# A block of attention, a token mixer and an MLP on one core: x's tile used again as room, and attention blocks normalised as each ends

## The chip, the core and the metric

The kernel runs on one core of one Trainium2 chip. Five engines work side by side: TensorE (PE in the profile, its weight loads PEld), VectorE (DVE), ScalarE (ACT), GpSimd (POOL) and SyncE (SP), which issues every DMA here. The metric is device time in microseconds (us), the median of several executions; lower is better.

## What is computed

The input x has 2048 tokens of 640 features. Two branches start from its layer norm xn, and both are added to x. All is float32.

```python
qkv = (xn @ wqkv)                       # 32 heads of 20 features
p = softmax(q @ k.T * 20 ** -0.5)       # per head, 2048 x 2048
a = (p @ v) @ wo
h = gelu(xn @ w1)                       # then four groups of columns shifted by +1, -1, +2, -2 tokens
x1 = x + shifted(h) @ w2
b = x1 + gelu(layernorm(x1) @ w3) @ w4  # 1536 hidden features
out = x + a + b
```

## The kernel before

The kernel is written through a planner of its own (class `Plan`): each helper records an operation with its cost, its key (when it is wanted) and what it depends on, and `schedule` then lays all operations on the engines. For TensorE the order is not left to the planner: the string `ORDER` has one letter for each of its 7058 steps, and says of which kind the next one is. The instructions of each engine and of SP's queue then run in that order; an instruction that waits holds up all that stand behind it on its engine.

**Attention (letters m, s, p).** Two heads are a pair, and a pair has two blocks of 1024 queries: 32 blocks (`blk`). A block is 32 units. `max_step` (m) makes scores of 128 queries against 512 keys for both heads, and DVE takes their maximum (`mx<-pm`); `max_fin` turns a block's maxima into two more rows of q's tile, by way of TensorE (`pmt`) and DRAM (`md`). `unit` (s) makes the transposed scores, two products of 62 rows that run side by side; ACT takes exp of each (`p<-s`); every second unit, (p) adds the four products of probabilities and values into `pv`. A quarter of a block's keys is summed in PSUM, copied out by ACT or DVE (`obq<-pv`) and added by POOL (`ob<-ob,obq`). m runs 43 units ahead of s. There are 1024 m, 1024 s and 512 p.

**Dense products (letter d).** All of the projections are filled in between: v, k and q (`psv`, `ps_k`, `ps_q`), w1 (`ps1`), w2 with the residual and the layer norm (`ps2`, transposes `tz`), w3 (`ps3`), w4 (`ps4`) and wo (`pso`, and `psl` for the last rows). Each float32 operand is split in a rounded part and a rest, so a product is three passes. `twins` runs two sums side by side in two halves of TensorE's rows, and changes halves in the middle; between the two turns `fence`, a POOL memset of one element (`scratch`, L334), waits for the last product of the first turn, and the first product of the second turn waits for it.

**Memory.** `xT` holds xn transposed, hi and lo, for all tokens (80 KB of each partition) until the last product of q and w1. `w23_phase` then opens new tiles: `w2s` (w2, later part of w4), `zT` (the second layer norm transposed, half of the tokens at a time, later the rest of w4), and `hs` with the shifted h. `w4_phase` splits a tile `g` of 128 tokens into `gT` for each of 16 sums `ps4_t`. When w4 is through, `wo_phase` opens `wos` (wo), `acc` (the result) and `oc`.

**End of a block.** `block_end` writes a block's sums `ob` to DRAM (`od`), copies the heads' rows to `onm` and the row of denominators to `sm`, takes their reciprocal (`rc<-sm`, DVE), and writes that back (`rcd`) and 20 times over (`rce`). `load_o` in `wo_phase` reads `onm` and `rce`, and POOL or DVE multiplies them (`oc<-oc,rb`).

Of the kernel before, what the change touches and what calls it, by code (L numbers as in the profile page):

```python
# [95 lines left out]
    "dddddddddddddddddddddddddddddddddddddddddddddddddddddddddddddddddddddddddddddddddddddddddddddddddddddddddddddm"  # L96
    "dddddddddddmddddddddddddddddddddddddddddddddddddddddddddddddmddddddddddmmdddddddmdddddmddddddddmddddddddddmddd"
    "ddmdmddddddddmddmddddddddddmdddddddddddmmddddddddddddddddmdmmddddddddddddddmddddddddddddmddddmmddddddddddmdddd"
    "dddddddmdddddmddddmmdddddddddddddddddmdddddmddddddddmmdddddddmddddddddddddmdddddddddmdddmmddddddddddddmddddddd"
    "mdddddddsddsddsdddddddddddddddddddsddddmsdddddddmssdddddddsddmddppppdsdddsddddsdddmdddsddmdddmsdddmdsddddmsddd"  # L100
    "dsdddmmppppmsdddmdmdsddddsddmdsdddsmddddsmddddsmddsddmdddmmppppsmddsddmdsddmddmdsdddmddsmdddddmddddsdmddsdmdmd"
    "dmppmspsmpsmsmssmpsmspsmspmmspsmspmmspsmddddsmddddmdddsdmdddsmdddsdmdddsdmdddsdmdddsppmsmpsmpmmspsdddmddsddddm"
    "dddddmdspdmsddddddmsddddsddmdddmppmdsddddddsddmddddddsmdddddsddmdddsdddddmmppmsddsddddmddsddddmdddsmdddddddsmd"
    "ddsdddddmmppppsmdddsddddmdsdddmddddsmddddddsdmdddsdddmddspmsmpppmsdddsddddmddsddddddsmddddsddmddsdddmddddsmppp"
    "pddssdmddddddddmsdddddmsdddddmddsddmddddmdmdppsmddddddsdmdddddsdmddsddmddddsddmdddddsdmdpssmpsdddmddsddmdddddd"
# [490 lines left out]
def tile_kernel(tc, x, wqkv, wo, w1, w2, w3, w4, out):  # L596
# [401 lines left out]
    def w23_phase():  # L998
# [4 lines left out]
        for k in range(ND):  # L1003
            load_row(w2s, "w2", k)
# [444 lines left out]
```

## Time and profile before

| | us |
|---|---|
| median of 3 runs | 1900.74 |
| the 3 runs | 1896.83 to 1901.31 |
| the profiled execution | 1897.56 |
| its span, first to last instruction | 1895.8 |

The profiled execution took 1.8 us more than its span, and 3.2 us less than the median. The page has busy times by engine and a strip of 40 slices; windows give the same for any stretch; a timeline has instructions in order of time. A busy PE is not PE at its best: a product's end is modelled, and a product that waits inside a run of others still counts as busy. So what PE could do is read from the distances between starts.

### The profile page before, as it was taken

The numbers are of one execution on the slowest core, as the hardware profiler recorded it, in microseconds if no ns is written. First come the engines' busy times: TensorE is split into PE (matmuls) and PEld (weight loads), VectorE is DVE, ScalarE is ACT, GpSimd is POOL, SyncE is SP. The second block draws the span as 40 slices with busy tenths as digits, with TensorE's granted clock in tenths as the row PEclk, the third lists the DMA queues.
The fourth block names the chain that finished last, engine by engine and source line by source line (L and its number), as shares of the span: only waits on it lengthen the run. The fifth ranks groups of instructions, "written<-read, shape, count | busy, mean of one in ns | idle before, by whom it ended". The sixth has DMA issues, their size and how long they took to land.

```text
span 1895.8 us, 44073 instructions
## 1 busy us (share of the span) xinstructions
PE 1871.9 (99%) x17185; PEld 1278.4 (67%) x17185; DVE 1581.2 (83%) x2826; ACT 1340.8 (71%) x2461; POOL 353.9 (19%) x562
## 2 busy tenths in 40 slices
PE   7999999999999999999999999999999999999998
PEld 5975666565656657676666756665777776775677
DVE  8979888888888989988788998778787888788734
ACT  4267767777877885777787667778577776767661
POOL 5001111212112112211112311111122112211221
PEclk9999999999999999999999999999999999999999
DMA  4554545655555466545346573435523232314612
GB/s 173 167 170 146 156 119 135 184 161 180 148 152 149 127 196 220 169 154 169 125 131 219 172 225 105 128 101 162 139 86 107 74 108 86 91 53 156 224 48 112
DMA packets 234375, 271.57 MB, mean 143 GB/s; under 512 B 59006, under 2 KB 174158, under 8 KB 232366
## 3 DMA queue, kind: packets, MB, share of 16 engines
q1 hardware_dynamic: 234166, 268.75, 46.4%
q8 instruction: 135, 2.21, 0.5%
q14 instruction: 74, 0.61, 0.1%
HBM read 162.72 MB, written 115.79 MB: 147 GB/s over the span
## 4 chain that ended last, share of the span: by engine, by line
PE 94%; DVE 3%; DMA 2%; POOL 1%; issue 1%; SPq 0%; ACT 0%; DVEq 0%; POOLq 0%; ACTq 0%
PE ps L346 26%; PE pv L346 24%; PE s L346 14%; PE pm L346 14%; PE psv L346 4%; PE pso L346 3%; PE ps_k L346 3%; PE ps_q L346 3%; DVE mx L316 2%; PE psl L346 1%; DMA wd_w<-ph_w 1%; PE tz L316 1%; PE tp L316 0%; DMA od<-ob 0%; PE pmt L346 0%
## 5 line engine op out<-in xcount | busy, mean ns | idle before, releaser
L316 DVE TENSOR_REDUCE mx<-pm 128x1 f32<-128x512 f32 x2048 | 1282.0, 683 | 195.6 <-PE pm L346 178.8
L316 ACT ACTIVATE p<-s 128x512 f32<-128x512 f32 x2048 | 1084.2, 609 | 293.4 <-PE s L346 249.8
L346 PE MATMUL pv<-p,v 128*32 128x512 f32 x4096 | 494.6, 598 | 0.0
L346 PE MATMUL s<-zq,kpack 62*128 62x512 f32 x2048 | 449.7, 413 | 3.8 <-DVE mx L316 1.5
L346 PE MATMUL pm<-kpack,zq 60*128 60x512 f32 x2048 | 450.6, 413 | 0.5
L346 PEld LDWEIGHTS s<-zq,kpack 62*128 62x128 f32 x2048 | 231.9, 185 | 133.7 <-DVE mx L316 40.9
L346 PEld LDWEIGHTS pm<-kpack,zq 60*128 60x128 f32 x2048 | 229.7, 185 | 124.9 <-DVE mx L316 35.4
L346 PEld LDWEIGHTS pv<-p,v 128*32 128x32 f32 x4096 | 109.6, 109 | 222.2 <-issue 193.2
L346 PE MATMUL ps<-zT,w_w 64*128 64x512 f32 x1440 | 228.6, 394 | 0.0
L316 POOL TENSOR_TENSOR ob<-ob,obq 128x512 f32<-128x512 f32 x96 | 125.0, 1302 | 414.4 <-ACT obq L316 311.1
L346 PEld LDWEIGHTS ps<-zT,w_w 64*128 64x128 f32 x1440 | 150.2, 186 | 21.0 <-POOL scratch L334 1.7
L346 PE MATMUL ps<-zT,gT 64*128 64x320 f32 x1344 | 140.0, 306 | 0.0
L346 PEld LDWEIGHTS ps<-zT,gT 64*128 64x128 f32 x1344 | 124.2, 186 | 4.8
L316 ACT COPY obq<-pv 128x512 f32<-128x512 f32 x77 | 45.2, 588 | 99.6 <-PE pv L346 98.3
L346 PE MATMUL ps<-w2s,gT 64*128 64x320 f32 x960 | 98.2, 307 | 0.0
L346 PE MATMUL ps<-w2s,hs 64*128 64x320 f32 x960 | 96.3, 309 | 0.0
L346 PE MATMUL psv<-wv,xT 64*128 64x320 f32 x960 | 94.6, 314 | 1.6 <-POOL wv L316 1.5
L346 PE MATMUL ps<-xT,w_w 64*128 64x512 f32 x600 | 95.5, 395 | 0.0
L334 POOL MEMSET scratch<- 1x1 f32 x134 | 11.9, 89 | 422.2 <-PE ps L346 227.1
L346 PEld LDWEIGHTS ps<-w2s,gT 64*128 64x128 f32 x960 | 85.3, 186 | 7.7 <-ACT p L316 0.8
L346 PEld LDWEIGHTS psv<-wv,xT 64*128 64x128 f32 x960 | 82.7, 189 | 9.3 <-POOL wv L316 2.2
L346 PEld LDWEIGHTS ps<-w2s,hs 64*128 64x128 f32 x960 | 84.5, 185 | 6.1 <-DVE mx L316 1.7
(173 smaller groups left out, 1498.1 us busy)
## 6 DMA issues: line engine op xcount, KB each, us to landing
zq<-qd SPq DMA_DIRECT2D x156, 80.0 KB
kpack<-kd SPq DMA_DIRECT2D x78, 160.0 KB
w_w<-wd_w SPq DMA_DIRECT2D x48, 256.0 KB
gd<-pre SPq DMA_DIRECT2D x8, 1536.0 KB
g<-gd SPq DMA_DIRECT2D x64, 192.0 KB
wd_w<-ph_w SPq DMA_DIRECT2D x34, 320.0 KB
vd<-vst SPq DMA_DIRECT2D x32, 256.0 KB
kd<-hl_k SPq DMA_DIRECT2D x16, 512.0 KB
```

Source lines behind the costliest of these rows:

```text
L316: getattr(e, m)(val(out), *[val(x) for x in ins], **{k: val(v) for k, v in kw.items()})
L334: o.insts = [nc.gpsimd.memset(scratch.get(), 0.0)]
L346: o.insts = [nc.tensor.matmul(out.get(), lhsT.get(), rhs.get(), **kw) for out, lhsT, rhs, kw in products]
```

## The change

Inputs, products and the number of steps of each kind in `ORDER` stay; the order itself is written anew. The edits are these.

- `xT` stays open to the end of w4. Its first 640 columns of tokens become w2 (`W2`) and later part of w4, the columns 640 to 896 the shifted h of every second pair of tiles, its second half z, the rest of w4 (`w4v`), and the split g of every odd w4 sum. `w2s` and `zT` are gone. For this, the last two dense jobs before w2 (`w1_4` and `q4`) run their halves crosswise, so that the first half of the tokens is read out earlier.
- 15 of w4's 24 pieces (10 before) are loaded ahead of the second half's w3. `g` has one buffer instead of two.
- Four fifths of wo (`wos`) are loaded into `g`'s place once the last g is split, ahead of the last w4 sum's result. The last fifth (`ws4`), `oc` and `acc` come after w4.
- `block_end` writes the four rows of denominators alone (8 KB), reads the reciprocals back spread over 32 partitions each (`rb`, 4 DMAs), POOL multiplies (`rb<-ob,rb`), and 4 DMAs write `onm`. `rce` and the 20 products `oc<-oc,rb` in `wo_phase` are gone.
- `place` and `vst` move to pools that close early.

```diff
-    place = const.tile([P, 2, 2, P], F32R, name="place")
+    lnp = pl.pool(name="lnp", bufs=2)
+    place = lnp.tile([P, 2, 2, P], F32R, name="place")
...
-    od = dt([NPAIR, 2, P, 512], F32, "od")
+    od = dt([NB, 4, 512], F32, "od")
     onm = dt([D, S], F32, "onm")
-    rcd = dt([NB, 2 * HALF], F32, "rcd")
-    rce = dt([D, S], F32, "rce")
+    rcd = dt([NB, 4, 512], F32, "rcd")
     r2d = dt([NT, P], F32, "r2d")
...
+                if room and turn + i == 0:
+                    last.deps.append((room.tile.alloc_op, 1))
...
+    vsp = pl.pool(name="vsp", bufs=1, side="right")
...
+        ends = []
+
+        def run(n, w):
+            f = w1_tile if n[0] == "w" else qk_tile
+            if n not in jobs[-2:]:
+                return f(n, w)
+            ends.append((f, n, w))
+            f(n, w, (0,))
+        ahead(jobs, lambda n: early(w1_load, n) if n[0] == "w" else early(wcol, st1, n), run)
+        for f, n, w in ends:
+            f(n, w, (2,))
         wp.close()
...
+    W2 = [[xT[:, :, k, 320 * n:320 * (n + 1)] for n in range(2)] for k in range(ND)]
+    ZC = S // 2
+    HS = slice(640, 896)
+
...
-        w2p = pl.pool(name="w2p", bufs=1, side="right")
-        w2s = w2p.tile([P, 2, ND, D], F32R, name="w2s")
-        wp = pl.pool(name="ztp", bufs=1, side="right")
-        zT = wp.tile([P, 2, ND, S // 2], F32R, name="zT")
...
+        def hs_load(q):
+            if q % 2 == 0:
+                hs = [xT[:, :, k, HS] for k in range(ND)]
+            else:
+                t = sp.tile([P, 2, ND, 256], F32R, tag="hs", name=f"hs{q}", bufs=1)
+                hs = [t[:, :, k, :] for k in range(ND)]
+            t0 = q * 256
+            edge = {0: 0, NT // 2 - 1: 254}.get(q)
+            for k in range(ND):
+                if edge is None:
+                    dma(_f(hs[k]), _f(hsd[k][:, :, t0:t0 + 256]), 262144)
...
-                pl.renew(w2s)
-                for k in range(ND):
-                    load_row(w2s, "w4", k)
-                gp = pl.pool(name="s4g", bufs=2, side="right")
-                gs = [load_g(gp, t) for t in range(2)]
+                xrp.close()
+                for key in W4_ALL[:3 * ND]:
+                    early(dma, _f(w4v(*key)), _f(wdone["w4_%d_%d" % key]), 327680)
+                gp = pl.pool(name="s4g", bufs=1)
...
+    def w4v(k, n):
+        i = 2 * (k - ND) + n
+        if k < ND:
+            return W2[k][n]
+        if i < ND:
+            return xT[:, :, i, 640:960]
+        i -= ND
+        return xT[:, :, i // 3, ZC + 320 * (i % 3):ZC + 320 * (i % 3 + 1)]
...
+            if t % 2:
+                gT = [[xT[:, p, 3 + k // 6, ZC + k % 6 * P:ZC + (k % 6 + 1) * P] for k in range(NF)] for p in range(2)]
+                split(xT[:, 0, 3:5, ZC:ZC + 768], xT[:, 1, 3:5, ZC:ZC + 768],
+                      g.rearrange("p (a k) t -> p a (k t)", a=2), NF * P)
+            else:
+                gt = sp.tile([P, 2, NF, P], F32R, tag="gT", name=f"gT{t}", bufs=1)
+                split(gt[:, 0], gt[:, 1], g, NF * P)
+                gT = [[gt[:, p, k, :] for k in range(NF)] for p in range(2)]
+            if t + 1 < NT:
+                gs.append(load_g(gp, t + 1))
+            else:
+                gp.close()
+                wp = pl.pool(name="wosp", bufs=1)
+                ws = wp.tile([P, 2, 4, D], F32R, name="wos")
+                for k in range(4):
+                    load_row(ws, "wo", k)
             pss = [pd(f"ps4_{t}_{n}")[:, :320] for n in range(2)]
...
+    def load_o(sp, k, b):
+        m = P if k < 4 else r0
+        oc = sp.tile([P, 512], F32, tag="oc", name=f"oc{k}_{b}", bufs=8)
+        if m < P:
+            pl("pool", 600.0, "memset", oc[64:], 0.0, port=True)
+        dma(oc[:m], onm[k * P:k * P + m, b * 512:(b + 1) * 512], m * 2048)
+        return oc
...
-            for c in range(0, HALF, 512):
-                rb = sp.tile([P, 512], F32, tag="rb", name=f"rb{k}_{half}_{c}", bufs=3)
-                dma(rb[:m], rce[k * P:k * P + m, half * HALF + c:half * HALF + c + 512], m * 2048)
-                pl("pool", c_pool(512), "tensor_mul", oc[:m, c:c + 512], oc[:m, c:c + 512], rb[:m], port=True,
-                   alt=("dve", c_dve(512), "tensor_mul", True))
...
-        adma(od[pair, qh], ob, 262144)
         n = 2 * HALF // P
-        cols = slice(qh * HALF, (qh + 1) * HALF)
-        src = od[pair, qh].rearrange("(q e r) n -> e r q n", e=2, q=2)
-        for e in range(2):
-            h = 2 * pair + e
-            adma(onm[h * DH:(h + 1) * DH, cols].rearrange("r (q n) -> r q n", q=2), src[e, :DH], 81920)
+        adma(od[blk], ob[DH:P:32, :], 8192)
         pl.key += REST
         sm = pp.tile([P, n], F32, tag="sm", name=f"sm{blk}", bufs=2)
-        adma(sm, od[pair, qh].rearrange("(s r) (c n) -> s r c n", r=32, n=n)[:, DH], 8192, LATE)
+        adma(sm, od[blk].rearrange("s (c n) -> (s c) n", n=n), 8192, LATE)
         rc = pp.tile([P, n], F32, tag="rc", name=f"rc{blk}", bufs=2)
         pl("dve", 185.0, "reciprocal", rc, sm)
-        adma(rcd[blk].rearrange("(p n) -> p n", n=n), rc, 8192)
-        src = rcd[blk].rearrange("(q e n) -> e q n", e=2, q=2)
-        for e in range(2):
-            h = 2 * pair + e
-            adma(rce[h * DH:(h + 1) * DH, cols].rearrange("r (q n) -> r q n", q=2),
-                 src[e].unsqueeze(0).to_broadcast([DH, 2, 512]), 81920)
+        adma(rcd[blk].rearrange("s (c n) -> (s c) n", n=n), rc, 8192)
+        rb = pp.tile([P, 512], F32, tag="rb", name=f"rb{blk}", bufs=1)
+        for r in range(4):
+            adma(rb[32 * r:32 * (r + 1), :], rcd[blk, r:r + 1].to_broadcast([32, 512]), 65536)
+        pl("pool", c_pool(512), "tensor_mul", rb, ob, rb, port=True)
+        for r in range(4):
+            h = 2 * pair + r % 2
+            c0 = qh * HALF + r // 2 * 512
+            adma(onm[h * DH:(h + 1) * DH, c0:c0 + 512], rb[32 * r:32 * r + DH, :], 40960)
```

Where the order moves, in the rows of the two built programs. TensorE first, around the end of w4's last sum, `ps4_15`, in the program before: the sum's last row, then attention alone (the number after s is the unit, after pm the step of maxima).

```order
L346 MATMUL ps4_15_0_27265<-zT_11047,gT15_26762 128x320
L346 MATMUL s939_0_27600<-zq2_81,kpack0_77 128x512
L346 MATMUL s939_1_27601<-zq2_81,kpack0_77 128x512
L346 MATMUL s940_0_27604<-zq2_81,kpack0_77 128x512
L346 MATMUL s940_1_27605<-zq2_81,kpack0_77 128x512
```

From here no dense row stands until wo's. In the program before, the same attention runs on to the first product with wo, `pso_0`. The last unit before it is 981, the last step of maxima 1018 (1019 stands two rows behind it).

```order
L346 MATMUL pv30_2_28324<-p978_0_28233,v15_26406 32x512
L346 MATMUL pv30_2_28324<-p979_0_28273,v15_26406 32x512
L346 MATMUL pv30_2_28324<-p978_1_28272,v15_26406 32x512
L346 MATMUL pv30_2_28324<-p979_1_28274,v15_26406 32x512
L346 MATMUL pso_0_0_28345<-wos_27719,oT0_0_27730 128x320
L346 MATMUL pso_0_1_28346<-wos_27719,oT0_0_27730 128x320
```

So 43 units, 939 to 981, stand between the two. The changed program at the end of `ps4_15`, which stands behind unit 942 there:

```order
L346 MATMUL ps4_15_0_27434<-xT_201 128x320
L346 MATMUL pm988_0_27803<-kpack1_77,zq0_78 128x512
L346 MATMUL pm988_1_27804<-kpack1_77,zq0_78 128x512
L346 MATMUL s943_0_27808<-zq2_80,kpack0_76 128x512
L346 MATMUL s943_1_27809<-zq2_80,kpack0_76 128x512
```

The sum has moved behind four more units. And the changed program at the first product with wo:

```order
L346 MATMUL pm1014_0_28422<-kpack1_77,zq1_79 128x512
L346 MATMUL pm1014_1_28423<-kpack1_77,zq1_79 128x512
L346 MATMUL s976_0_28433<-zq0_78,kpack1_77 128x512
L346 MATMUL s976_1_28434<-zq0_78,kpack1_77 128x512
L346 MATMUL pso_0_0_28438<-wos_26986,oT0_0_27942 128x320
L346 MATMUL pso_0_1_28439<-wos_26986,oT0_0_27942 128x320
```

Between the two sums stand 43 s, 32 m and 22 p before, and 34 s, 27 m and 20 p now.

POOL at the end of block 20, before: the last two quarters are added, and two fences and the first quarter of block 21 follow.

```order
L316 TENSOR_TENSOR ob20_18747<-ob20_18747,obq20_2_19898 128x512
L316 TENSOR_TENSOR ob20_18747<-ob20_18747,obq20_3_20021 128x512
L334 MEMSET scratch_67 1x1 x2
L316 TENSOR_TENSOR ob21_19500<-ob21_19500,obq21_1_20179 128x512
L316 TENSOR_SCALAR nm_22_19160<-m8_22_19148 128x16
L316 CAST hr_22_19161<-nm_22_19160 128x16
```

Nothing of block 20 is left to POOL after that until `wo_phase`. And now, for block 20: the product `rb20` stands behind the quarters with a fence ahead of it and one behind it.

```order
L316 TENSOR_TENSOR ob20_19044<-ob20_19044,obq20_2_20020 128x512
L316 TENSOR_TENSOR ob20_19044<-ob20_19044,obq20_3_20136 128x512
L334 MEMSET scratch_67 1x1
L316 TENSOR_TENSOR rb20_19849<-ob20_19044,rb20_19849 128x512
L334 MEMSET scratch_67 1x1
L316 TENSOR_TENSOR ob21_19793<-ob21_19793,obq21_1_20294 128x512
```

Of the 30 products `rb`, 6 have a fence as the next instruction of POOL and 4 more as the next but one.

SP's queue near the end of w4, before: the last result of w4 (`ad` from `r15`) is written, then wo is loaded.

```order
L316 DMA ad_123<-r14_26519 128x640
L316 DMA od_128<-ob28_25644 128x512
L316 DMA onm_129<-od_128 20x2x512 x2
L316 DMA sm28_25785<-od_128 128x1x16
L316 DMA rcd_130<-rc28_25822 128x16
L316 DMA rce_131<-rcd_130 20x2x512 x2
L316 DMA ad_123<-r15_26892 128x640
L316 DMA wos_27719<-wd_wo_0_0_327 128x2x320
L316 DMA wos_27719<-wd_wo_0_1_328 128x2x320
```

All of wo stands behind the results of w4. Now wo's loads stand ahead of the results of sums 14 and 15 (`r15` is only being loaded), and behind block 27's new chain of DMAs, of which the first two rows show the end.

```order
L316 DMA rb27_26066<-rcd_125 32x512 x4
L316 DMA onm_124<-rb27_26066 20x512 x4
L316 DMA ad_118<-r13_26172 128x640
L316 DMA wos_26986<-wd_wo_0_0_327 128x2x320
L316 DMA wos_26986<-wd_wo_0_1_328 128x2x320
L316 DMA wos_26986<-wd_wo_1_0_329 128x2x320
L316 DMA wos_26986<-wd_wo_1_1_330 128x2x320
L316 DMA wos_26986<-wd_wo_2_0_331 128x2x320
L316 DMA wos_26986<-wd_wo_2_1_332 128x2x320
L316 DMA wos_26986<-wd_wo_3_0_333 128x2x320
L316 DMA wos_26986<-wd_wo_3_1_334 128x2x320
L316 DMA r15_27071<-rd_117 128x640
```

Eight loads of wo (four fifths of it) have moved ahead of `r15`; each needs the place of the last g, so SP waits there until g15 is split.

## Rows read from the trace of the kernel before

**Rows 1.** The page: span, busy times, strip of PE's clock, chain.

```profile
span 1895.8 us, 44073 instructions
...
PE 1871.9 (99%) x17185; PEld 1278.4 (67%) x17185; DVE 1581.2 (83%) x2826; ACT 1340.8 (71%) x2461; POOL 353.9 (19%) x562
...
PEclk9999999999999999999999999999999999999999
...
PE 94%; DVE 3%; DMA 2%; POOL 1%; issue 1%; SPq 0%; ACT 0%; DVEq 0%; POOLq 0%; ACTq 0%
```

**Rows 2.** Windows of four stretches, products of s alone: window, length, PE busy (count).

```profile
646.40:657.00 10.60, 3.44 (x12) 1.00 0.51 112
...
1106.20:1118.10 11.90, 4.63 (x22) 1.00 0.86 182
1298.50:1322.40 23.90, 8.45 (x32) 1.00 0.62 213
1721.50:1773.40 51.90, 20.72 (x86) 1.00 0.73 248
```

**Rows 3.** Timeline of PE in the last stretch: start, length, what.

```profile
1747.95 0.39 PE L346 MATMUL pm<-kpack,zq 60*128 60x512 f32 x2
1748.18 0.40 PE L346 MATMUL s<-zq,kpack 62*128 62x512 f32 x2
1748.51 1.06 PE L346 MATMUL pv<-p,v 128*32 128x512 f32 x8
1749.50 0.50 PE L346 MATMUL pm<-kpack,zq 60*128 60x512 f32 x2
```

**Rows 4.** Timeline of PE while w4 runs.

```profile
1500.76 3.64 PE L346 MATMUL pv<-p,v 128*32 128x512 f32 x32
1504.33 0.50 PE L346 MATMUL pm<-kpack,zq 60*128 60x512 f32 x2
```

**Rows 5.** Groups in the stretch 1721.5 to 1773.4: busy us, mean ns | idle before.

```profile
L316 ACT ACTIVATE p<-s 128x512 f32<-128x512 f32 x85 | 43.5, 635 | 6.8 <-PE s L346 5.6 <-PE pv L346 0.8
L316 DVE TENSOR_REDUCE mx<-pm 128x1 f32<-128x512 f32 x65 | 40.2, 680 | 6.8 <-PE pm L346 6.8
L346 PE MATMUL pv<-p,v 128*32 128x512 f32 x176 | 22.4, 602 | 0.0
...
L346 PE MATMUL pm<-kpack,zq 60*128 60x512 f32 x64 | 16.8, 454 | 0.0
```

**Rows 6.** Windows of that stretch and the next: PE, PEld, DVE, ACT, POOL busy.

```profile
1721.50:1773.40 51.90, 51.86 (x330) 20.95 (x326) 44.87 (x77) 46.13 (x92) 8.44 (x10) 1.00 0.73 248
1773.40:1825.30 51.90, 51.90 (x607) 42.31 (x604) 29.41 (x54) 28.13 (x56) 15.83 (x24) 1.00 0.38 129
```

**Rows 7.** Groups of DVE in the same stretch.

```profile
L316 DVE TENSOR_TENSOR oc<-oc,rb 128x512 f32<-128x512 f32 x3 | 2.0, 683 | 0.0
```

**Rows 8.** Groups of POOL over the whole span.

```profile
L316 POOL TENSOR_TENSOR ob<-ob,obq 128x512 f32<-128x512 f32 x96 | 125.0, 1302 | 414.4 <-ACT obq L316 311.1 <-DVE obq L316 94.7 <-DVE ph_wo L316 8.1
L316 POOL TENSOR_TENSOR gT<-g,gT 128x1536 fp32r<-128x1536 f32 x12 | 41.8, 3484 | 136.2 <-ACT gT L316 85.9 <-DMA zq<-qd 28.2 <-DMA g<-gd 11.6
...
L334 POOL MEMSET scratch<- 1x1 f32 x134 | 11.9, 89 | 422.2 <-PE ps L346 227.1 <-PE psv L346 43.6 <-PE pso L346 36.1
```

**Rows 9.** Waits of SP's queue: total, times, longest us.

```profile
SPq L316 <- DMA rcd<-rc: 33.6, 22, 6.2
```

**Rows 10.** Waits of the engines: total, times, longest us.

```profile
POOL scratch L334 <- PE ps L346: 227.1, 48, 18.2
```

**Rows 11.** The page: weight loads of w3's sums, with PE's wait for fences.

```profile
L346 PEld LDWEIGHTS ps<-zT,w_w 64*128 64x128 f32 x1440 | 150.2, 186 | 21.0 <-POOL scratch L334 1.7
```

**Rows 12.** Timeline of DVE and POOL side by side.

```profile
1752.79 1.29 DVE L316 TENSOR_REDUCE mx<-pm 128x1 f32<-128x512 f32 x2 [1.46 <-PE pm L346]
1752.88 1.28 POOL L316 TENSOR_TENSOR ob<-ob,obq 128x512 f32<-128x512 f32 x1 [7.30 <-ACT obq L316]
```

**Rows 13.** Groups of ACT over the whole span.

```profile
L316 ACT CAST gT<-g 128x1536 fp32r<-128x1536 f32 x14 | 20.8, 1482 | 2.0 <-PE ps L346 2.0
```

More of the change, by code (lines that the diff above doesn't have):

```diff
@@ L101 @@
[L101 to L105, printed above, removed]
@@ L708, in parts, with twins @@
         return [(lhs(a, k), rhs(b, k)) for k in kts for a, b in ((0, 0), (0, 1), (1, 0))]
-    def twins(tiles, sums, n, first=0, more=()):
+    def twins(tiles, sums, n, first=0, more=(), room=None):
         last = None
@@ L810, in tile_kernel @@
     vw0 = v_load(0)
-    vst = [pp.tile([P, 8, 2, VC], F32, name=f"vst{i}", tag=f"vst{i}", bufs=1) for i in range(VSB)]
+    vst = [vsp.tile([P, 8, 2, VC], F32, name=f"vst{i}") for i in range(VSB)]
     wvr = [v.rearrange("p a b c -> p (a b c)")[:, :320] for v in vst]
@@ L924, in ahead, with qk_tile @@
             run(n, cur)
-    def qk_tile(nm, w):
+    def qk_tile(nm, w, ts=(0, 2)):
         dst = (qd, kd)["qk".index(nm[0])][int(nm[1])]
-        for t2 in range(0, 4, 2):
+        for t2 in ts:
             pss = [pd(f"ps_{nm}_{tb}") for tb in (t2, t2 + 1)]
@@ L965, in w1_load, with w1_tile @@
             return w
-        def w1_tile(nm, w):
+        def w1_tile(nm, w, ts=(0, 2)):
             c = int(nm[3:])
-            for t2 in range(0, 4, W1B):
+            for t2 in ts:
                 pre = wp.tile([P, 512 * W1B], F32, tag="pre", name=f"pre1_{c}_{t2}", bufs=W1N)
@@ L1110, in w4_phase @@
+    W4_ALL = [(k, n) for k in range(NF) for n in range(2)]
+    def w4_phase(gp, gs):
+        fill["part"] = "w4"
+        sp = pl.pool(name="s4p", bufs=1, side="right")
+        for key in W4_ALL[3 * ND:]:
+            early(dma, _f(w4v(*key)), _f(wdone["w4_%d_%d" % key]), 327680)
         for t in range(NT):
             g = gs[t]
-            r = sp.tile([P, D], F32, tag="r", name=f"r{t}")
-            dma(r, rd[t * P:(t + 1) * P, :], 327680)
-            gT = sp.tile([P, 2, NF, P], F32R, tag="gT", name=f"gT{t}", bufs=2)
@@ L1128, in w4_phase, with wo_phase @@
         sp.close()
-        gp.close()
-        zp.close()
-        w2p.close()
-    def wo_phase():
+        xtp.close()
+        return wp, ws
+    r0 = (H - 2) * DH - 4 * P
+    def load_o(sp, k, b):
[5 more added lines that the diff above has]
+        return oc
+    def wo_phase(wosp, ws):
@@ L1147, in wo_phase @@
                       _f(wdone[f"wo_4_{n}"][r0 + i % 2 * DH:r0 + (i % 2 + 1) * DH]), 51200)
+        for n in range(2):
+            dma(_f(ws4[:, :, 0, 320 * n:320 * (n + 1)]), _f(wdone[f"wo_4_{n}"]), 327680)
         acc = wp.tile([P, NT, D], F32, name="acc")
@@ L1205, in wo_phase @@
         wp.close()
+        wosp.close()
     v_half(0, *vw0)
@@ L1212, in tile_kernel @@
     v_half(1, *vw)
+    vsp.close()
     key = pl.key
@@ L1420, in tile_kernel @@
     tick(0.0)
-    wo_phase()
+    wo_phase(*wo_ws)
     with tc.manual_schedule():
```

244 lines of the change are left out of this document (113 added, 131 removed).

## Prediction

> **What bounds the kernel now.** The page comes first. TensorE is busy for 99% of the span, its clock is granted in full, at its upper level, in all 40 slices, and 94% of the chain that ended last lies on it [rows 1]. So time can come only from TensorE: from products that it no longer makes, from changes between kinds of product, or from waits inside the busy time. The change makes the same products (12632 of the row kind, 2180 of the column kind, 177 of full size, in both programs), so the first is nothing.
>
> For the third I read distances between starts. In attention alone, a pair of pm is followed by a pair of s 0.23 us later, and the next pair by pv 0.33 us later: the step into pv costs 0.10. One pv group (8 products) lasts 0.99 to the next start, four last 3.57 [rows 3, 4]: each further group is 0.86, so 0.13 of the 0.99 is the step out. Now the same in windows. Between two dense sums of different stages the program has stretches of attention alone, where TensorE lives on what ACT (exp) and DVE (maxima) leave it. The longest goes from 1721.5 to 1773.4: 86 products of s [rows 2], 64 of pm, 176 of pv [rows 5], which is 75 pairs and 22 groups in 17 runs. At the distances above that is 75 x 0.235 + 22 x 0.86 + 17 x 0.23, with 0.2 for one pmt 40.7 us; the stretch took 51.9, so 11.2 us went by in waits. ACT is busy for 46.1 of the 51.9 and DVE for 44.9, against 28.1 and 29.4 in the 51.9 us behind it, where wo's sums stand between [rows 6]. ACT is the slower: two exps of 0.635 are 1.27 us a unit [rows 5].
>
> The same sum for all eight stretches in which over 1 us is lost (four of them with length and products of s are in [rows 2]; the rest is read from the same view, and the pairs of m, the groups and the runs are counted in the program's order): 158.1 (15 s, 14 m, 10 groups, 9 runs) 2.4 us; 646.4 (6, 8, 5, 3) 2.3; 682.6 (25, 20, 16, 14) 4.1; 785.9 (9, 4, 5, 4) 1.4; 988.2 (19, 16, 12, 10) 4.8; 1106.2 (11, 7, 6, 6) 1.2; 1298.5 (16, 13, 12, 8) 4.7; 1721.5 (43, 32, 22, 17) 11.2. Together 32.1 us over 144 units, 0.22 a unit. This is where the kernel can be bettered; elsewhere dense rows fill what ACT and DVE leave.
>
> **The change part by part.** *The order of TensorE.* In the changed program the eight stretches hold 13, 4, 25, 8, 17, 8, 14 and 34 units: 123, 21 fewer. The nine of the last come from wo being there when its sums may start (its loads stand ahead of the last results of w4), two from q4's and w1_4's halves run crosswise. The units are not gone; they stand between dense rows, where ACT and DVE are free for over 40% of the time [rows 6]. At 0.22 each, 21 are 4.7 us. The bounds: by the stretch with the least loss for a unit (1.2 over 11) 2.3 us, by the one with the most (2.3 over 6) 8.0. I take 4.7, since the last stretch, with 9 of the 21, has 0.26, near the mean.
>
> *Changes of kind.* The order has 541 changes between row, column and full products; it had 556. Five of the runs of column products are gone, but four of those stood in the eight stretches, where TensorE waits anyway. One run at 0.23 and five changes to or from full at about 0.1 are 0.8 us, at least 0, at most 1.7 (15 at 0.115).
>
> *wo_phase.* Three of the products oc<-oc,rb ran on DVE in the last stretch, 2.0 us [rows 7]; they and the loads of rce are gone. DVE is not the slower engine there, so I count 0.5 us, between 0 and 2.0.
>
> *block_end.* 30 products of 128x512 on POOL are new. By the sums ob<-ob,obq of the same size one is 1.30 us [rows 8], 39 us in all; POOL is busy for 19% of the span [rows 1], so the time itself is free. The wait is not: the product stands in POOL's queue until rb has landed, four DMAs after od. SP waited for the landing of rcd, the step just ahead, 22 times, 1.5 us on average and 6.2 at most [rows 9]. So a product may hold POOL for 1.5 + 1.3 = 2.8 us. Queued behind are fences (134 in 1896 us), the sums ob and nm. Of the 30, ten have a fence as POOL's next instruction or next but one. If all of these were due just then, TensorE would lose 28 us. But POOL now mostly stands at a fence before TensorE gets there: it waited 227 us in 48 waits for ps, 4.7 us each on average [rows 10], more than 2.8; and TensorE's loads for w3 were kept by scratch for 1.7 us in the whole run [rows 11]. I count a quarter of one such hold, 0.7 us, with 0 and 28 as ends.
>
> *At nothing.* The one buffer for g: g of the next sum loads once this one is split, and a sum has some 25 us (16 of them stand between the ends of the last two stretches, 1322.4 and 1721.5 [rows 2]), while a split is 1.48 on ACT and 3.48 on POOL [rows 8, 13]; if the load were late, up to that much would show at each sum. SP's wait for g's place ahead of wo holds r15, md and zq of block 29 behind it; all are wanted many units later. w4's late loads are nine instead of fourteen, behind a stretch that is bound by ACT. place and vst move to pools that close where the old ones did. SP issues 110 DMAs more of some 1400, but od, onm and rce shrink.
>
> *The sum.* 4.7 + 0.8 + 0.5 - 0.7 = 5.3 us. Against the profiled execution's 1897.6 that is 1892.3; against the median, 3.2 higher, 1895.4. I give 1893.5, between the two. The likeliest case by itself reaches from 1887.5 (8.0 + 1.7 + 2.0 off 1899.2, midway between execution and median) to 1898. About 0.3% (5.7 us) is what a measurement here can tell from no change, so my sum lies just at that edge.
>
> **The rivals.**
>
> *Nothing gained.* The exps that leave the stretches have to be made somewhere; if ACT's 0.635 us were the limit behind them too, the waits would only move there. For it: ACT is busy for 71% of the whole span, DVE for 83% [rows 1]. Against it: in the stretch behind, ACT is busy 28.1 of 51.9 us [rows 6]. The time would be that of before, 1896 to 1901.
>
> *POOL's new product holds the fences: slower.* The price is up to 2.8 us for each of ten. It decides from four full holds on: 11.2 us, 5.9 more than the 5.3 gained. From there on the time is 1905 to 1915. For it: rb is read under traffic, and SP's longest wait of this kind was 6.2 us [rows 9]. Against it: POOL's 4.7 us of standing ahead.
>
> *The shared way to memory.* POOL's products could also slow DVE. In the trace two maxima took 1.29 us beside a POOL sum of 1.28 [rows 12], 0.65 each, no more than the mean 0.68 [rows 5]. So the maxima, 80% of DVE's work, aren't touched; for the rest, a fifth of 39 us is 8 us of DVE, with slack nearly everywhere: 1893 to 1901. The Trainium skill, SBUF — State Buffer, section "SBUF: two separate sides", speaks against the change here: DVE and GpSimd share a pair of ports as an exclusive lock, and who comes second waits for the whole instruction, where DVE's operation has two operands in SBUF or runs in a fast mode. By that rule the trace agrees for the maxima, which have one operand, in PSUM; if it held for every DVE operation, all 39 us would be lost and the time be some 1932.
>
> *The split into xT waits.* Odd sums' g goes into the tile from which TensorE reads w4 in that very moment. If the split had to wait for the sum before, each of eight sums would start later by 1.48 + 3.48 us [rows 8, 13], 40 us: 1933. The regions don't overlap, so I give it little.
>
> **How the numbers follow.** The stretches shorten as counted 0.63, of which 0.42 beyond 0.3% (the sum is at the edge, and its terms reach further up than down); nothing gained 0.20; fences held 0.09; ports 0.03; split waits 0.02; something in the start or the tail that is not priced here 0.03, to either side. Faster by over 0.3% is 0.44, within 0.3% 0.41, slower 0.15. For eight in ten the range goes from 1885 (the lower end of the likeliest, with some 2 us for stages that I don't price) to 1903, which takes in the nothing-gained case and the mildest of held fences.
>
> **What the profile after would show.** Right: TensorE at 99%; the stretch between ps4_15 and pso about 43 us long, with 68 products of s and some 8 to 9 us of waits; rb<-ob,rb at 1.30 us x30; waits for scratch by TensorE under 3 us. Wrong: pso or ps2 waiting for a DMA or oT ahead of its first product; POOL idle before rb for more than 3 us a block and TensorE's rows behind fences starting late; gaps at the start of odd ps4 sums. What would make it wrong most easily is waits in the dense stages of which no row of before tells: 5 us are 5 ns for each of a thousand units.

## The result

| | median, us | runs | mean granted clock |
|---|---|---|---|
| before | 1899.34 | 10, 1894.9 to 1904.6 | |
| changed | 1904.55 | 10, 1901.3 to 1911.1 | 0.997 |

The ratio is 1.0032, with a 95% interval of 1.0016 to 1.0048: the changed kernel is slower by 5.2 us, where 5.3 us less were forecast, and its median lies above the stated range of 1885 to 1903. In a later comparison (f0 below) the ratio was 1.0038 (1.0023 to 1.0052). Two executions of later comparisons, one of before at 2649 us and one of g4 at 3580 us, are left out of the ratios and mean clocks.

**The page.** Of the changed kernel: the engines' busy times, the strip of the granted clock, the chain's shares and the new product's group.

```profile
PE 1867.2 (98%) x17185; PEld 1280.4 (67%) x17185; DVE 1576.3 (83%) x2827; ACT 1333.0 (70%) x2443; POOL 395.9 (21%) x599
...
PEclk9999999999999999999999999999999999999999
...
PE 87%; DMA 5%; DVE 4%; ACT 2%; issue 1%; SPq 1%; POOL 1%; DVEq 0%; POOLq 0%; ACTq 0%
...
L316 POOL TENSOR_TENSOR rb<-ob,rb 128x512 f32<-128x512 f32 x30 | 39.2, 1306 | 169.7 <-DMA rb<-rcd 157.6
```

Against [rows 1], TensorE is busy for 4.7 us less and yet the kernel is longer, and 5% of the chain are DMAs. The new product costs 39.2 us of POOL as priced, but POOL stood idle ahead of the 30 of them for 169.7 us, 5.7 each. Now the waits (us in total, times, longest):

```profile
POOL rb L316 <- DMA rb<-rcd: 157.6, 26, 13.9
...
PE ps L346 <- POOL scratch L334: 2.7, 1, 2.7
...
DVE oT L316 <- DMA oc<-onm: 2.2, 1, 2.2
...
ACT oT L316 <- DMA oc<-onm: 1.9, 1, 1.9
```

SP's queue stands for the product too, ahead of the four stores that write it out:

```profile
SPq L316 <- POOL rb L316: 61.5, 23, 3.8
```

A hold, in what follows, is an instruction that waits at the head of its engine's queue while others that are ready stand behind it.

**The first hold, at 352 us.** POOL's timeline (start, length, engine, line, operation, idle time ahead and what ended it), and TensorE's at the same place:

```profile
335.33 0.87 POOL L316 TENSOR_TENSOR ph_w<-pr_w,ph_w 128x320 fp32r<-128x320 f32 x1 [8.03 <-ACT ph_w L316]
347.90 1.29 POOL L316 TENSOR_TENSOR rb<-ob,rb 128x512 f32<-128x512 f32 x1 [11.70 <-DMA rb<-rcd]
349.15 0.86 POOL L316 TENSOR_TENSOR ph_w<-pr_w,ph_w 128x320 fp32r<-128x320 f32 x1
349.97 2.49 POOL L316 TENSOR_TENSOR hlh<-pre,hlh 128x512 fp32r<-128x512 f32 x2
352.39 0.09 POOL L334 MEMSET scratch<- 1x1 f32 x1
```

```profile
349.38 0.49 PE L346 MATMUL pm<-kpack,zq 60*128 60x512 f32 x1
352.53 0.74 PE L346 MATMUL ps<-xT,w_w 64*128 64x512 f32 x4 [2.66 <-POOL scratch L334]
```

The product of block 3 kept POOL for 11.7 us of standing and 1.3 of work. Three operations stood behind it, and behind these the fence for which TensorE's next turn of `ps1` waits: between the starts of two products lie 3.15 us, of which TensorE stood idle for 2.66.

**The second hold, at 1751 us.** This is in the stretch of attention alone ahead of `pso`. First DVE and ACT, then TensorE:

```profile
1749.20 0.69 DVE L316 COPY obq<-pv 128x512 f32<-128x512 f32 x1
1752.10 0.43 DVE L316 CAST oT<-oc 128x512 fp32r<-128x512 f32 x1 [2.20 <-DMA oc<-onm]
1752.44 3.67 DVE L316 TENSOR_REDUCE mx<-pm 128x1 f32<-128x512 f32 x6
```

```profile
1753.11 0.62 ACT L316 CAST oT<-oc 128x512 fp32r<-128x512 f32 x1 [1.89 <-DMA oc<-onm]
1753.63 1.57 ACT L316 ACTIVATE p<-s 128x512 f32<-128x512 f32 x3
```

```profile
1751.36 0.49 PE L346 MATMUL s<-zq,kpack 62*128 62x512 f32 x1
1753.18 0.49 PE L346 MATMUL s<-zq,kpack 62*128 62x512 f32 x1 [1.32 <-DVE mx L316]
```

In the program before, the product by `rb` took the wait for such a load, and in this stretch that was POOL, which had time:

```profile
1766.26 1.28 POOL L316 TENSOR_TENSOR oc<-oc,rb 128x512 f32<-128x512 f32 x1 [12.10 <-DMA rb<-rce]
```

Without these products, the casts of wo's operand are the first to wait for the load, in the queues of DVE and ACT, ahead of the maxima and exps on which TensorE lives there. The load was late, and all three engines stood. What came next is in the windows (busy time of each engine, then the granted clock, DMA share and GB/s):

```profile
1732.40:1776.00 43.60, 42.17 (x289) 15.95 (x287) 36.47 (x63) 36.60 (x73) 11.80 (x13) 0.96 0.65 217
...
1750.60:1754.00 3.40, 1.97 (x12) 0.55 (x4) 1.90 (x4) 1.51 (x4) 2.04 (x3) 1.00 0.97 273
1754.00:1757.50 3.50, 3.50 (x15) 1.03 (x14) 2.20 (x5) 1.72 (x5) 1.11 (x1) 0.51 1.04 391
1757.50:1761.00 3.50, 3.50 (x28) 1.24 (x28) 2.76 (x5) 3.33 (x8) 0.00 (x0) 1.00 1.03 400
```

Right after the wait the clock is granted at its lower level (1.2 GHz) for 3.4 us, a dip: 15 products where the next 3.5 us have 28. In before's trace the clock falls only in the kernel's last microseconds. The strip of the page doesn't show it: a slice is 47 us, and with 3.4 of them at half clock it is still a 9.

**Where the time went.** The start of the same product of s (numbered in the order of TensorE), in four traces (g1 is the kernel below with both holds moved):

| product of s | before | changed | changed again (f0) | g1 |
|---|---|---|---|---|
| 128 | 210.1 | 210.3 | 210.4 | 210.7 |
| 256 | 317.8 | 322.1 | 322.2 | 322.1 |
| 288 | 350.1 | 353.1 | 353.0 | 349.1 |
| 416 | 460.3 | 465.5 | 465.3 | 462.0 |
| 704 | 702.3 | 711.5 | 712.4 | 708.2 |
| 832 | 821.6 | 833.4 | 836.1 | 830.1 |
| 928 | 906.9 | 919.5 | 922.3 | 918.8 |
| 1088 | 1045.4 | 1056.8 | 1059.6 | 1056.0 |
| 1856 | 1697.2 | 1706.9 | 1709.8 | 1706.2 |
| 1984 | 1801.1 | 1806.5 | 1809.5 | 1802.5 |

At 128, 416, 832 and 1856 both programs have made the same number of products of every kind ahead of the one in the row; at 256 the changed one has made 22 more and at 288 10 fewer, elsewhere the counts differ by up to 8. So the 4.3 us at 256 are mostly other work: at products 244 and 264, with equal counts, the lag is 1.4 and 1.5 us.

The changed kernel falls behind by 12 us between 210 and 835 us, and gets 4.3 back across the stretch ahead of `pso` (9.7 behind at product 1856, 5.4 at 1984). Between places with equal counts the lag of the changed trace grows by 1.4 us ahead of 231 us of before's time, by 2.7 at the first hold, by 1.4 from there to 486 us, by 4.0 between 608 and 697 us, and by 2.4 between 734 and 799 us. The largest step, at 608 to 697 us, is 4.1 us in g1 and 5.0 in f0. There the halves of `q4` and `w1_4` run crosswise and SP issues the first loads of w2 and h into `xT`'s place.

### The profile page after: what moved, and what is told of

It is laid out like the page before. It is cut to its first block, busy times and chain, and to the rows that moved or that the text cites. A ratio compares the mean times of both kernels' runs of the same rounds, so it can differ in the third digit from the quotient of the medians.

```text
span 1900.7 us, 44369 instructions
## 1 busy us (share of the span) xinstructions
PE 1867.2 (98%) x17185; PEld 1280.4 (67%) x17185; DVE 1576.3 (83%) x2827; ACT 1333.0 (70%) x2443; POOL 395.9 (21%) x599
## 4 chain that ended last, share of the span: by engine, by line
PE 87%; DMA 5%; DVE 4%; ACT 2%; issue 1%; SPq 1%; POOL 1%; DVEq 0%; POOLq 0%; ACTq 0%
PE ps L346 25%; PE pv L346 22%; PE pm L346 13%; PE s L346 13%; PE psv L346 4%; PE pso L346 3%; PE ps_q L346 3%; PE ps_k L346 3%; DVE mx L316 2%; SPq L316 1%; PE psl L346 1%; ACT p L316 1%; DMA sm<-od 1%; DMA zq<-qd 1%; DMA xT<-hsd 1%
## 5 line engine op out<-in xcount | busy, mean ns | idle before, releaser
L346 PE MATMUL ps<-xT,w_w 64*128 64x512 f32 x2040 | 323.8, 395 | 2.7 <-POOL scratch L334 2.7
L346 PEld LDWEIGHTS ps<-xT,w_w 64*128 64x128 f32 x2040 | 213.1, 186 | 37.9 <-POOL scratch L334 5.5
L346 PE MATMUL ps<-xT 64*128 64x320 f32 x1632 | 169.0, 307 | 0.0
L346 PEld LDWEIGHTS ps<-xT 64*128 64x128 f32 x1632 | 150.0, 186 | 6.9 <-POOL scratch L334 0.4
L346 PE MATMUL ps<-xT,gT 64*128 64x320 f32 x1152 | 121.9, 307 | 0.0
L346 PEld LDWEIGHTS ps<-xT,gT 64*128 64x128 f32 x1152 | 108.5, 186 | 6.1 <-DVE mx L316 0.8
L346 PE MATMUL ps_q<-xT,w_q 64*128 64x512 f32 x480 | 77.8, 396 | 0.1
L346 PE MATMUL ps_k<-xT,w_k 64*128 64x512 f32 x480 | 77.0, 394 | 0.1
L316 POOL TENSOR_TENSOR rb<-ob,rb 128x512 f32<-128x512 f32 x30 | 39.2, 1306 | 169.7 <-DMA rb<-rcd 157.6
```

The lines of the kernel that those rows point to most:

```text
L316: getattr(e, m)(val(out), *[val(x) for x in ins], **{k: val(v) for k, v in kw.items()})
L346: o.insts = [nc.tensor.matmul(out.get(), lhsT.get(), rhs.get(), **kw) for out, lhsT, rhs, kw in products]
```

## The experiments

Theory 1 at the start: the product rb<-ob,rb holds POOL's queue, 8 to 11 us. Rival 2: the new order or loads cost it. Rival 3: the clock's dips do. Theory 4, from g1 on, takes 1 and 3 together: late DMAs hold in-order queues, and the clock dips behind a hold in a stretch of attention alone. The mean clock is that of all runs of a kernel. The e runs, the f runs, g1 with g2, g3 with g4, and h1 are on five chips, each beside before on its own chip.

| run | ratio to before, 95% | median, before beside it | mean clock, before's |
|---|---|---|---|
| e1 product later, planned anew | 1.0108 (1.0090 to 1.0127) | 1921.3, 1900.1 | 0.9946, 0.9987 |
| e2 product without its wait, planned anew | 1.0065 (1.0052 to 1.0078) | 1913.4, 1900.1 | 0.9957, 0.9987 |
| e3 old block end | 1.0101 (1.0087 to 1.0115) | 1919.9, 1900.1 | 0.9948, 0.9987 |
| e4 old order string | 1.0199 (1.0186 to 1.0212) | 1938.5, 1900.1 | 0.9925, 0.9987 |
| f0 the changed kernel again | 1.0038 (1.0023 to 1.0052) | 1908.8, 1902.0 | 0.9959, 0.9986 |
| f1 same order, no wait | 1.0018 (1.0002 to 1.0034) | 1904.4, 1902.0 | 0.9962, 0.9986 |
| f2 same order, all products later | 1.0042 (1.0027 to 1.0057) | 1909.4, 1902.0 | 0.9959, 0.9986 |
| g1 both holds moved | 0.9991 (0.9978 to 1.0004) | 1900.2, 1901.7 | 0.9982, 0.9982 |
| g2 and three casts | 0.9999 (0.9985 to 1.0012) | 1901.3, 1901.7 | 0.9978, 0.9982 |
| h1 second hold alone moved | 1.0023 (1.0012 to 1.0034) | 1902.7, 1899.6 | 0.9974, 0.9990 |
| g3 g1 and two casts | 0.9980 (0.9964 to 0.9996) | 1899.1, 1901.7 | 0.9983, 0.9985 |
| g4 g3 and hl_q4_2 | 0.9982 (0.9963 to 1.0000) | 1898.8, 1901.7 | 0.9985, 0.9985 |

**e1 to e4: edits that the planner lays out anew.**

```diff
# e1
-            adma(rb[32 * r:32 * (r + 1), :], rcd[blk, r:r + 1].to_broadcast([32, 512]), 65536)
+            adma(rb[32 * r:32 * (r + 1), :], rcd[blk, r:r + 1].to_broadcast([32, 512]), 65536, RBLATE)   # 8000.0
# e2: ahead of the four loads of rb
+        pl("pool", c_pool(512), "tensor_mul", rb, ob, ob, port=True)
-        pl("pool", c_pool(512), "tensor_mul", rb, ob, rb, port=True)
# e3: block_end, od, rcd, rce and the products in load_o as before
# e4: ORDER as before
```

> The changed kernel, with the landing of rb planned 8 us later, so that each of POOL's 30 products rb<-ob,rb is placed one or two instructions later in POOL's order (behind the split or fence that stood behind it); TensorE's order is the same but for four rows. Theory 1 (the product's wait for rb in POOL's queue holds the fences and sums behind it, some 8 to 11 us between 230 and 835 us): POOL's waits for rb fall from 157.6 us to some 30 (what is over 8 us in nine of the 30 waits), TensorE's waits in 225 to 850 us fall with them, and the time to 1891 to 1896. Rival 2 (the new order of TensorE, or the new routes of loads, cost it; the product is hidden): the waits fall just so, the time moves by under 2 us, 1902 to 1906. Rival 3 (TensorE's clock, granted at its lower level in a dip of the last attention-only stretch): unchanged too, and the dip is still there.

> The changed kernel, with POOL's 30 products made from ob and ob in place of ob and rb, ahead of rb's landing (leaves out the normalisation by rb: what is stored in onm is rb itself). The same 30 products of 128x512 and the same DMAs, but none stands in POOL's queue for a DMA. Theory 1: like the experiment with the later product or better, 1889 to 1895, since 39 us of POOL's work alone cost nothing. If POOL's work or the shared memory port were the cost and not the wait: no change, 1902 to 1906. Rival 2: 1902 to 1906 as well; the two are told apart by leaving the product out.

> The changed kernel with the block end of before: od whole, onm by two copies in memory, rce spread by two DMAs, and the 15 products by rb in front of wo (on POOL or DVE) in place of the 30 at the blocks' ends. TensorE's order stays that of the changed kernel but for some 17 rows. Theory 1: the loss of 225 to 850 us goes, some of the gain at wo goes too (0.5 to 2 us): 1892 to 1898. Rival 2: 1902 to 1907.

> The changed kernel with the order string of before (kinds of product on TensorE, 2580 of 14833 rows elsewhere); buffers, loads and block ends are those of the change. Theory 1: the loss stays (the product still waits for rb) and the gain of the shorter stretches goes: 1904 to 1912. Rival 2, if it is the new order that costs: 1895 to 1900; if it is the new routes of loads: 1904 to 1912 like theory 1, and then the three other runs decide.

All four are slower, by more than any theory allowed. In e1 the waits for rb went as expected, and the wait at 352 us with them (from product 256 to 288 of s it gains 3.1 us on the changed kernel):

```profile
POOL rb L317 <- DMA rb<-rcd: 10.9, 3, 8.1
```

But the planner had laid some 60 rows of POOL, 60 of DVE and 100 of SP in another order, while the order string stayed, and TensorE met new waits, such as this one at 703 us and three more of 2.0 to 2.4 us (at 752, 1143 and 1370 us):

```profile
703.14 1.32 PE L347 MATMUL pm<-kpack,zq 60*128 60x512 f32 x4 [2.12 <-DMA xr<-in_A_x_dram]
```

So these runs don't tell the theories apart. They suggest that a string of kinds goes with one layout of the other engines (with the string of before it is 1938), and that a single edit has to be made behind the planner.

**f0, f1, f2: the order of every engine kept.** In f1 only the emitted instruction differs; in f2 the products, with the four stores that need them, are put later in the finished list.

```diff
# f1
-        pl("pool", c_pool(512), "tensor_mul", rb, ob, rb, port=True)
+        o = pl("pool", c_pool(512), "tensor_mul", rb, ob, rb, port=True)
+        o.fn = lambda: nc.gpsimd.tensor_mul(ob.get(), ob.get(), ob.get())
# f2, g1 to g4, h1: emit() moves single operations of the finished list behind
# what was planned up to so many ns later and does not need them
+        order = self.schedule()
+        for m in self.late:
...
+            order[n:n + k] = go + back
```

> The changed kernel once more, beside the two others on one chip, for its trace in another execution. By rival 3 (TensorE's clock granted at its lower level for some us after a wait in a stretch of attention alone) an execution at 1904 to 1906 us shows more such dips than the one at 1902.5, whose records had one of 3.4 us inside the kernel; by theory 1 alone every execution shows the same waits and no more dips. Time 1902 to 1907.

> The changed kernel with the order of every engine as it is, row for row; only POOL's 30 products read ob twice in place of ob and rb, into ob (leaves out the normalisation by rb: rb itself is stored in onm). Work and DMAs are those of the change, but none of the 30 stands in POOL's queue for a DMA. The earlier runs had the planner lay all engines out anew, so that other waits came with the edit; here nothing else can move. Theory 1, as it stands now (the product's wait holds what is behind it in POOL's queue): the 3.2 us wait of TensorE at 352.5 us, for a fence behind rb3, goes, and the time falls by 3 to 9 us to 1896 to 1901. Rival 2 (the wait is hidden but for that one place, and the rest of the loss comes from elsewhere in the new order): 1900 to 1903. Rival 3 (clock): the dip in the last attention-only stretch stays, since none of its waits is for POOL.

> The changed kernel as planned, in which each product rb<-ob,rb, with the stores behind it, is put 8 planned us later once the plan is made: 28 of 30 move behind one to six of POOL's instructions (64 in all), SP's stores with them, nothing else moves on any engine. The output is the full one. Theory 1: POOL's waits for rb fall from 157.6 us to under 30, the wait at 352.5 goes, and the time is within 2 us of the run without the wait, 1896 to 1902. If it is the plan that has to fit the string of kinds and not the hold: no gain, 1902 to 1907.

f1's median is 4.4 us below f0's on the same chip, but by the spread of the 12 and 8 executions that may be anything from some 0.4 to 8.5 us. In f0 TensorE waits for the fence at 352 us, in f1 it doesn't:

```profile
PE ps L346 <- POOL scratch L334: 2.8, 1, 2.8
```

2.9 us of the gain show at this place in f1's trace (its product 256 of s starts 2.4 us after f0's, and 288 0.5 us ahead). With the products' waits f1 also takes away SP's wait for them, and its product of one tile with itself takes 1.05 us, not 1.29. So the 4.4 us are the price of the waits as far as these two were of no account.

f2 gains 2.7 us at 352 us and ends no faster: its trace has 1.7 us more at the first product of s, and waits of 1.8 to 1.9 us with dips at 748 and 813 us, which f1 doesn't have. f0 has the second of them too, and f1 has four other dips, so one trace of each doesn't explain f2's time. Moving 28 products moves SP's stores too; which of these moves costs what f2 gains at 352 us stays open. f0's trace has two dips inside the kernel (809 and 1757 us), the first trace had one.

**g1, h1: the two places that the change made.**

```diff
+MOVES = (("pool", "rb3", 8000.0),
+         ("dve", "oT0_2", 6000.0),
+         ("act", "oT0_3", 6000.0),)
# h1: without the first
```

> The changed kernel as planned, with three instructions put later once the plan is made: POOL's product rb3<-ob3,rb3 (behind four more of POOL's instructions), DVE's cast oT0_2<-oc2_0 and ACT's cast oT0_3<-oc3_0 (each behind some eight maxima or exps). They are the two places at which the change itself put an instruction that waits for a DMA in front of work that TensorE needs: 352.5 us (3.2 us of TensorE's wait) and 1753 us (DVE stood 2.20 us and ACT 1.89 us for oc<-onm, TensorE 1.6 us, and the clock then stood at its lower level for 3.4 us). Theory 4 (holds by late DMAs in in-order queues, with the clock's dip behind those that fall into a stretch of attention alone): both waits and the dip at 1753 go, 5 to 7 us, ratio to before from 1.0032 to 1.0038 down to 0.9995 to 1.0015 (1899 to 1903). If the waits only move on to the next thing that is late: above 1.0025.

> The changed kernel as planned, with only DVE's cast oT0_2<-oc2_0 and ACT's cast oT0_3<-oc3_0 put later; POOL's product rb3 stays where it is. In the run without the products' wait the time fell by 4.4 us against the changed kernel on the same chip (1908.8 to 1904.4), 3.3 of them at equal granted clock, and with both holds moved by 8.6. If the two holds add up and the second one costs mostly by the clock: the wait of 3.2 us at 352.5 us stays, the stretch ahead of pso has no dip and is some 40 us long instead of 43.7, the mean granted clock rises from 0.996 to 0.998, and the time is 3 to 5 us below the changed kernel, ratio to before 1.0010 to 1.0022. If the clock's dips come elsewhere whatever the stretch does: ratio above 1.0025 with the clock at 0.996 to 0.997.

POOL and DVE in g1, where the product now stands behind the fence and the cast behind eight maxima:

```profile
345.88 2.54 POOL L320 TENSOR_TENSOR hlh<-pre,hlh 128x512 fp32r<-128x512 f32 x2 [1.26 <-ACT hlh L320]
348.42 0.09 POOL L339 MEMSET scratch<- 1x1 f32 x1
348.60 1.29 POOL L320 TENSOR_TENSOR rb<-ob,rb 128x512 f32<-128x512 f32 x1
```

```profile
1749.33 5.10 DVE L320 TENSOR_REDUCE mx<-pm 128x1 f32<-128x512 f32 x8
1755.02 0.69 DVE L320 TENSOR_REDUCE mx<-pm 128x1 f32<-128x512 f32 x1 [0.59 <-PE pm L351]
1755.63 0.42 DVE L320 CAST oT<-oc 128x512 fp32r<-128x512 f32 x1
```

The fence comes at 348.4 and not 352.4, DVE has no wait, and the stretch is 40.4 us long with the clock in full (g1's window, then h1's):

```profile
1731.70:1772.10 40.40, 40.11 (x290) 15.22 (x288) 36.43 (x63) 36.60 (x73) 11.01 (x13) 1.00 0.67 219
```

```profile
1733.50:1773.90 40.40, 40.12 (x290) 15.19 (x289) 36.44 (x63) 36.65 (x73) 11.47 (x13) 1.00 0.67 222
```

Three instructions, put later, take the ratio from 1.0038 to 0.9991, a step of 0.47% where the two intervals together are about 0.2% to either side. The other 29 products still wait in g1, and this costs nothing that the time shows (g1's page):

```profile
L320 POOL TENSOR_TENSOR rb<-ob,rb 128x512 f32<-128x512 f32 x30 | 39.2, 1307 | 162.8 <-DMA rb<-rcd 143.2
```

In h1 the first hold is still there (POOL idle for 12.5 us, TensorE for 2.4 us at 351 us), the second is gone. Against 1.0038, the casts alone are worth 0.15%, the products' waits alone (f1) 0.20%: each of these by itself is no larger than the noise of such a difference (0.2%), and their sum agrees with the 0.47% within it. The traces are clearer on the second hold. The casts stand for `oc` in the changed kernel, f0, f1, f2 and e1, TensorE is idle there for 1.2 to 1.8 us, and in each of the five a dip comes next. With the casts moved, in g1 to g4 and h1, there is neither the wait nor a dip behind 1700 us. From product 1864 to 1974 of s, with equal counts at both ends, g1 and h1 gain 7.4 us on before's trace, and the changed kernel 4.2.

**g2, g3, g4: other casts that stand for a DMA.**

```diff
# g2; g3 without the last; g4 with 1000.0 in the last
+         ("act", "ph_k3_2", 4000.0),
+         ("act", "ph_w3_2_0", 4000.0),
+         ("act", "hl_q4_2", 2000.0),
```

> As the kernel with the two holds moved, and three more casts of ACT put later, at the other places where the trace of the changed kernel has ACT standing for a DMA while TensorE waits for what is behind it: ph_k3_2<-pr_k3_2 (229 us, ACT stood 3.50 us, TensorE 1.1), ph_w3_2_0 (450 us, 2.31 and 1.7) and hl_q4_2<-ps_q4_2 (696 us, 2.13 and 0.7 + 1.2). Theory 4: another 3 to 5 us, with the dips that other executions show at 232, 453 and 703 us gone too: ratio 0.997 to 1.000, so no slower than before and perhaps faster. If the loss is spread over many short waits: no more than 1 us below the other.

> The changed kernel with the two holds moved and the two casts ph_k3_2 (behind one more of ACT's instructions and one of DVE's) and ph_w3_2_0 (behind four), without the move of hl_q4_2, behind which the trace of the kernel with five moves shows a wait of TensorE of 2.9 us at 694 us (in place of 1.3 and 0.7) and a dip of the clock. Theory 4: it keeps the 2.1 us gained at 230 and 450 us and loses nothing at 694: 1 to 3 us below the kernels with two and with five moves, ratio to before 0.9975 to 0.999 (1896 to 1899). If moves that go well in one trace only shift the waits: 0.999 to 1.001.

> As the kernel with four holds moved, and ACT's cast hl_q4_2 put behind the two exps that follow it and no further (DVE's half of the split stays where it is), so that those exps no longer stand behind the landing of hsd<-hlh (2.1 us). Theory 4: TensorE's waits of 1.3 and 0.7 us at 694 to 696 us shrink to under 1 us together: 0.5 to 2 us below the kernel with four moves, ratio 0.997 to 0.9985. If the split's second half, on DVE in front of a maximum, is what TensorE waits for: no change, or the wait of the five moves again.

In g2's trace the waits at 230 and 450 us are gone (2.0 us against g1 by product 448), and the move of hl_q4_2 made a wait of 2.8 us at 694 with a dip behind it. Without that move g3 is 0.2% faster than before (0.04 to 0.36%), but its ratio and g1's differ by less than their intervals, so the 2.0 us stand in a trace and not in the times. g4 did not do what it was to: two waits of some 1 us each and a dip remain at 694 us, and its time is that of g3.

## Why the prediction was wrong

**What held.** The bound, and the stretch: 68 products of s, 43.6 us. By the distances of the prediction its 61 pairs and 20 groups in 19 runs need 36.1 us, so 7.5 us are lost (8 to 9 were forecast, 11.2 before). That the 43 us of the forecast came true is luck: 1.7 of the 7.5 are the dip and 1.3 the wait ahead of it, which the forecast didn't have. With the second hold away the stretch is 40.4 us, or 4.3 us of waits: the gain at this place was forecast too small, not too large, and the rival that the exps only move their waits elsewhere fails here. rb<-ob,rb took its 1.31 us 30 times. Shared ports didn't show: the 2048 maxima take 683 ns each in both traces. Nor did waits at the odd ps4 sums: TensorE is idle for 0.2 us between 1200 and 1600 us. (Of column and full products the traces count 4360 and 193, not 2180 and 177, but the same in both programs.)

**The step that failed** is "So a product may hold POOL for 1.5 + 1.3 = 2.8 us", and the "quarter of one such hold, 0.7 us" made from it. The 1.5 was SP's wait for one DMA of the chain [rows 9]. What POOL waits for is the end of the whole chain against the place that the planner gave the product, and four DMAs and DVE's reciprocal lie between: from the issue of od to the product's end it took 14 to 29 us in the 30 blocks. POOL stood 5.7 us on average and 13.9 at most. Seven of the 30 products stood for more than 10 us, far over the 4.7 us that POOL is ahead of TensorE [rows 10]. It was only behind block 3's, with three operations in between, that a fence came late for TensorE. The products' waits measured 4.4 us (f1 against f0, with the wide interval given there), where 0.7 were counted; the trace of the changed kernel has 2.7 of it at the one fence. This was the rival with 0.09, with one long hold instead of four short ones.

**What had no term.** In *wo_phase* I counted the products that go, and not that the casts behind them become the first to wait for `oc`: in-order queues again, now DVE's and ACT's, in the stretch where nothing covers them. Taken away alone it is 0.15%, 2.9 us, by the medians, and 3.2 us in the traces (7.4 against 4.2 above).

The clock had no term either: it was granted in full in all 40 slices of before [rows 1], so I gave it nothing. Over all runs, (1 - mean clock) x time is 7.9 us for f0 and 2.7 for before beside it: 5.2 of the 6.8 us between them. For g1 it is 3.3, and 3.4 for before. That is clock not granted, an upper measure of what TensorE lost by it. For f1 it is still 7.2, so the first hold costs by the wait and hardly by the clock: its 2.4 to 2.8 us of idle time in the changed kernel, f0 and h1 are followed by no dip in any of the three. For h1 it is 4.9, and 1.9 for before beside it.

Most dips follow a wait: in the thirteen traces of changed kernels and experiments I count 34 of them inside the kernel, of 3.41 or 6.83 us, and in the 4 us ahead of 30 the records have a gap of 1.0 us or more on TensorE (27 of 1.0 to 2.8 us, three of 3.1 to 7.1); four have a shorter one or none, such as one at 1324 us in f1. But not every wait brings one: of 54 such gaps between the first 60 and the last 30 us, 30 were followed by a dip within 4.5 us. The Trainium skill, TensorE: Matmul & The Clock Gate, section "HAM oscillation — how this bites in real kernels", says that a wait for a DMA in each tile of a loop, of some 3 to 5 us there, lets the gate fall back to half rate, so that the next tile starts slow. The trace agrees at 1754 us that the clock falls behind a wait, but the wait was shorter, 1.3 us, and TensorE waited for DVE, which stood for the DMA.

**The sum with what was measured.** The forecast was 5.3 us less. With both holds away the changed kernel is 1.5 us below before (g1, 1900.2 against 1901.7, not clear of no change), with two more casts moved 2.6 (g3). So by the medians even the mended change gives at most half of the forecast. The rest lies ahead of 930 us: g1 is 8.5 us behind before's trace at product 832 of s, with the same products made, and 11.3 at 934, where the same holds. Behind 930 us it gets nearly all of this back, more than the forecast had for the stretches there. So what failed beside the two holds is that the change was taken to cost nothing ahead of 930 us; the prediction's last sentence had named waits in the dense stages, of which no row of before tells, as the easiest way to be wrong. In g1's records TensorE is idle for 8.7 us between 200 and 1000 us, in before's for 2.5. Waits of 0.7 to 1.7 us at 230, 447, 694, 740, 802 and 907 us make up most of it; moving the first two gave 2.0 in a trace. Which edit brings the others and the loss at 608 to 697 us (the new order, the crosswise halves, the loads of w2 and h into xT's place) stays open: the old order doesn't fit the new program (e4), and the new order in the old program wasn't tried.

That the waits at 352 and 1751 us are a matter of the place of three instructions is shown by f1, h1 and g1. That the dips make up most of what the two cost together is argued from the mean clocks, and holds for the second alone; no run keeps a wait and takes its dip away.

## What to carry to other kernels

Price a new instruction that waits for a DMA by the end of its whole chain against its place in an in-order queue, take the longest case and not the mean, and name for each engine what stands behind it; this holds too for an instruction that comes to the front because another was removed. In a stretch where one engine lives on two others, a wait of 1 to 2 us may cost the clock as well, so look for the longest wait in such a stretch. Compare two orders of the same work only where both have made the same products. To test one place of a planned program, change the finished order and leave the planner out.

## What the hardware showed that was not expected

One wait of 1.3 us on TensorE, in 43.6 us in which it was otherwise busy, was followed by 3.4 us at the lower clock, while the longer one of 2.7 us at 352 us in the same trace was not. Executions of one program differ along with this: the ten first runs of the changed kernel go from 1901.3 us at a mean clock of 0.999 to 1911.1 at 0.995, with a correlation of -0.8 between time and mean clock.
